# mLSTM attention with a mixture of experts: a unit's router logits move behind the scores of the iteration in which its rows are turned

## The chip, the cores and the metric

The kernel runs on one core of a Trainium2 chip. The metric is the device time of one execution in microseconds (us); runs of the same kernel differ by about two per cent, so medians are given with their spread.

## The reference

```python
for t in range(S):                       # B, H, S, D = 4, 8, 768, 40
    m_new = np.maximum(f[t] + m, i[t])
    f_stab, i_stab = np.exp(f[t] + m - m_new), np.exp(i[t] - m_new)
    C = f_stab * C + i_stab * outer(v[t], k[t]);  n = f_stab * n + i_stab * k[t];  m = m_new
    y[t] = sigmoid(o[t]) * (C @ q[t]) / max(abs(n @ q[t]), 1)
x = y as 3072 rows of 320 columns
noisy = x @ w_gate + log1p(exp(x @ w_noise)) * noise       # 8 experts
top2 = the two largest of each row; top2_w = softmax over the two
out[row] += top2_w * (relu(x[row] @ w1[e]) @ w2[e])        # for both experts e of a row
```

The recurrence is computed in chunks of 64 steps as scores, masked weights and a carried state.

## The kernel before, in words

**Attention.** The work is cut into NU = 24 units; a unit gives 128 rows of x. A loop runs over iterations i = 0 to 21, and the last two units are written out behind it. In iteration i, DVE makes `kd` (L340) and `p`, scores times weights (L346), of unit i+1; PE makes the state (`c_part`, L360), the output (`o_part`, L369) of unit i and the exponents of the weights of unit i+2 in two halves (`e_part`, L308), which ACT takes through exp (L311). `f_part` (L374 to L381) divides and gates unit i's output into `XR` on DVE and POOL. PE turns the rows of unit i-1 (`t_part`, L392, into the PSUM bank `xt`), ACT copies them to SBUF (`tc_part`, L396, tile `xts`), and PE makes the scores of unit i+2 (`s_part`, L329 and L332).

**Logits.** `l_part` (L412) multiplies a unit's turned rows with the router's weights, into columns of the same bank `xt`; `lc_part` (L461) copies the 16 logits of each row out of it on ACT.

**Routing.** Four units are a group; there are six. When a group's last logits are there, `route` starts `g_part`, a Python generator that emits the routing steps: noise and top two (L486 to L537), ranks inside an expert (`r_part` on PE, L421 to L423, copied by L464), places (L559 to L598), one-hot tiles `ob` (L604, eight for a group), and from them a burst of eight matmuls (`b_part`, L432) that adds the group's tokens to the token table (L439 or L442). `fill` decides how many steps of it go on DVE in each iteration; ranks and burst are due a fixed count of `unit` later (`lag`). Engines run their instructions in the order written. When three groups are in the table, `decode` (L448 to L452) makes the list of tokens for the first part of expert 0, and POOL gathers their rows (L743); after five groups that of the second part, after six that of the third and of expert 1.

**Experts.** Expert 0 is done in three parts as its tokens become known. `mm1` (L955) makes 128 hidden columns in a block, eight blocks for a part; ACT writes the relu (`hh`, L966), DVE the residue of its rounding (`hlo`, L967). `mm2` (L980 to L982) makes 128 rows of output from eight times three matmuls, one of the three with `hlo`. In the eight blocks of the first part ACT and POOL also split w2 (L756, L757), and the logits of the last units, their ranks and bursts are slipped in between (`advance`). `transpose_x` (L773 to L777) turns gathered rows. From expert 1 on, no routing is left.

## Time and profile before

| | us |
|---|---|
| median of three runs | 547.19 |
| lowest, highest | 539.72, 549.98 |
| the profiled execution, device time | 542.42 |
| its span, first to last instruction | 540.6 |
| PE busy, share of the span | 514.9, 95% |
| DVE busy, share of the span | 356.4, 66% |

The profiled execution lies between the lowest and the middle run. The page puts 71% of the chain that ended last on PE and 13% on DVE. PE's busy time is modelled for pipelined matmuls, so a high share does not say that PE is at its peak.

### The profile page before, as it was taken

To read this page: it belongs to the slowest core of one execution; us is meant where nothing else is said; L and a number is where in the kernel's file an instruction comes from. 1 tells how busy PE (TensorE), PEld (TensorE's weight loads), DVE (VectorE), ACT (ScalarE), POOL (GpSimd) and SP (SyncE) were. 2 spreads that over 40 slices of the span, in tenths; PEclk is the share of its full clock that TensorE was granted. 3 is DMA by queue.
4 is the path that set the end of the run, shared out by engine and by line. 5 is a ranking of instruction groups with operands and counts; after the bars stand their busy time and mean duration, and the time that the engine had idled before them with its cause. 6 is when DMAs were issued, how large, how long until landed. Compare 5 with 4: busy or idle time off the path is not lost.

```text
span 540.6 us, 13450 instructions
## 1 busy us (share of the span) xinstructions
PE 514.9 (95%) x5151; PEld 484.0 (90%) x5152; DVE 356.4 (66%) x956; ACT 248.7 (46%) x611; POOL 244.5 (45%) x329
## 2 busy tenths in 40 slices
PE   7999999999979899999999999999999999999992
PEld 3788888878978897899999999999999999999992
DVE  8898999998786368674675485467548537546310
ACT  7588878967532145451543254154326315515200
POOL 7446775644352854325705632570562345151042
PEclk9599999997989999999999999999999999999997
DMA  5889987788675455239417714941861583272032
GB/s 140 191 234 231 241 218 214 198 240 217 238 245 164 91 65 139 79 68 277 106 31 200 170 51 86 264 96 34 233 133 44 130 221 85 56 165 26 2 40 37
DMA packets 49990, 77.04 MB, mean 143 GB/s; under 512 B 10201, under 2 KB 39408, under 8 KB 49920
## 3 DMA queue, kind: packets, MB, share of 16 engines
q1 hardware_dynamic: 38848, 57.38, 37.6%
q0 software_dynamic: 11072, 18.74, 19.1%
q8 instruction: 42, 0.69, 0.5%
q14 instruction: 28, 0.23, 0.1%
HBM read 52.50 MB, written 17.48 MB: 129 GB/s over the span
## 4 chain that ended last, share of the span: by engine, by line
PE 71%; DVE 13%; DMA 5%; issue 3%; POOL 2%; ACT 2%; another core or an unknown queue 1%; SPq 1%; POOLq 0%; DVEq 0%
PE s L955 21%; PE e L955 11%; PE o L982 5%; PE o L980 5%; PE o L981 5%; PE st L980 4%; PE st L982 4%; PE st L981 4%; PE o L369 2%; DMA raw<-w_in 2%; DVE ob L604 2%; PE e L308 2%; DVE p L346 1%; PE s L332 1%
## 5 line engine op out<-in xcount | busy, mean ns | idle before, releaser
L1006 POOL DMA_INDIRECT y_out<-y,tok x54 | 88.7, 1643 | 191.7 <-DVE y L996 188.9
L966 ACT ACTIVATE hh<-s 128x384 fp32r<-128x384 f32 (+3 forms) x91 | 42.5, 469 | 84.7 <-PE s L955 75.8
L955 PE MATMUL s<-xh,w1h 128*128 128x384 f32 (+6 forms) x273 | 77.4, 338 | 0.1
L743 POOL DMA_INDIRECT xg<-rows,tok x54 | 60.9, 1127 | 26.0 <-issue 14.9
L967 DVE SCALAR_TENSOR_TENSOR hlo<-s,hh 128x384 fp32r<-128x384 f32 (+3 forms) x91 | 47.5, 522 | 28.5 <-ACT hh L966 25.1
L955 PE MATMUL s<-xh,w1l 128*128 128x384 f32 (+6 forms) x273 | 61.9, 335 | 0.0
L980 PE MATMUL o<-w2h,hh 128*128 128x320 f32 x192 | 59.5, 310 | 1.9 <-ACT hh L966 1.9
L982 PE MATMUL o<-w2h,hlo 128*128 128x320 f32 x192 | 59.2, 308 | 0.7 <-DVE hlo L967 0.7
L981 PE MATMUL o<-w2l,hh 128*128 128x320 f32 x192 | 58.7, 306 | 0.0
L980 PE MATMUL st<-w2h,hh 128*128 128x320 f32 x168 | 51.9, 309 | 0.0
L982 PE MATMUL st<-w2h,hlo 128*128 128x320 f32 x168 | 51.7, 307 | 0.0
L981 PE MATMUL st<-w2l,hh 128*128 128x320 f32 x168 | 51.4, 306 | 0.0
L955 PEld LDWEIGHTS s<-xh,w1h 128*128 128x128 f32 x273 | 49.2, 188 | 1.6 <-ACT xh L775 0.4
L955 PEld LDWEIGHTS s<-xh,w1l 128*128 128x128 f32 x273 | 47.8, 188 | 1.0
L955 PE MATMUL s<-xl,w1h 128*128 128x384 f32 (+6 forms) x182 | 46.3, 335 | 0.2 <-DVE xl L776 0.2
L996 DVE TENSOR_SCALAR y<-o,gw 128x320 f32<-128x320 f32 x24 | 13.2, 550 | 45.4 <-PE o L982 43.4
L966 ACT ACTIVATE hh<-e 128x384 fp32r<-128x384 f32 (+3 forms) x45 | 21.2, 472 | 40.6 <-PE e L955 40.1
L381 POOL TENSOR_TENSOR xr<-tm,vk 128x320 f32<-128x320 f32 x24 | 20.9, 872 | 40.0 <-PE e L308 8.4
L955 PE MATMUL e<-xh,w1h 128*128 128x384 f32 (+6 forms) x135 | 38.6, 340 | 0.3 <-DVE hlo L967 0.2
L996 DVE TENSOR_SCALAR y<-st,gw 128x320 f32<-128x320 f32 x21 | 11.6, 551 | 41.1 <-PE st L982 41.1
L980 PEld LDWEIGHTS o<-w2h,hh 128*128 128x128 f32 x192 | 36.0, 188 | 2.7 <-ACT hh L966 2.5
L982 PEld LDWEIGHTS o<-w2h,hlo 128*128 128x128 f32 x192 | 36.0, 188 | 1.1 <-DVE hlo L967 0.9
(233 smaller groups left out, 1323.0 us busy)
## 6 DMA issues: line engine op xcount, KB each, us to landing
vk<-vk_in SPq DMA_DIRECT2D x48, 242.0 KB
raw<-w_in SPq DMA_DIRECT2D x7, 1280.0 KB
qk<-qk_in SPq DMA_DIRECT2D x48, 160.0 KB
raw<-w_in SPq DMA_DIRECT2D x7, 1024.0 KB
y_out<-zrow SPq DMA_DIRECT2D x15, 320.0 KB
raw<-w_in SPq DMA_DIRECT2D x18, 256.0 KB
xt__2859<-xb SPq DMA_DIRECT2D x36, 72.0 KB
rows<-xr POOLq DMA_DIRECT2D x12, 160.0 KB
```

Source lines behind the costliest of these rows:

```text
L308: T.matmul(ps, LE[j][0:KE, c, 64 - 64 * p:192 - 64 * p], RE[j][0:KE, p, :, c * L:c * L + L], start=True, stop=True)
L369: T.matmul(OQ[u][half[p], h, :], PP[u][n, p, h, :], VK[u % 4][p][n, h * 41:h * 41 + 41], start=True, stop=True)
L381: P.tensor_mul(XR[u], tm.rearrange("p h d -> p (h d)"), SG[u % 4])
L743: P.indirect_dma_start(out=XG[0:rows_of(e, t), t], out_offset=None, in_=XD[0:n], in_offset=bass.IndirectOffsetOnAxis(ap=token(e, t), axis= ...
L955: T.matmul(ps[:, 0:n], l, r, start=i == 0, stop=i == len(ops) - 1)
L966: A.activation(hi, x, AF.Relu)
L967: V.scalar_tensor_tensor(lo, x, 0.0, hi.bitcast(F32), op0=OP.max, op1=OP.subtract)
L980: T.matmul(ps, HH[:, j, c], W2H[:, j], start=j == 0, stop=False)
L981: T.matmul(ps, HH[:, j, c], W2L[:, j], start=False, stop=False)
L982: T.matmul(ps, HLO[:, j, c], W2H[:, j], start=False, stop=j == 7)
L996: V.tensor_scalar(y[0:n], ps[0:n], GW[e][0:n, t:t + 1], None, op0=OP.mult)
L1006: st = P.indirect_dma_start(out=out, out_offset=bass.IndirectOffsetOnAxis(ap=token(e, t), axis=0), in_=y[0:n], in_offset=None, compute_op= ...
```

## The change: what it does

A unit's logits are made one iteration sooner. Before, iteration i made the logits of unit i-2, ahead of the turning of unit i-1; now it makes those of unit i-1, behind that turning, its copy and the scores of unit i+2. The ranks and bursts stay ahead of the turning. `route` starts a group one iteration sooner. Behind the loop, the logits of unit 21 stand where unit 22 is turned, those of unit 22 behind the first block of mm1 and those of unit 23 behind its fourth block instead of its third.

```diff
     def l_part(i):
-        t = XTB if i < NU else psum.tile([128, 512], F32, name="st")
-        u = i - 2
+        t = XTB if i < NU - 1 else psum.tile([128, 512], F32, name="st")
+        u = i - 1
...
     def lc_part(i, t, w):
-        u = i - 2
+        u = i - 1
...
     def route(i):
-        if 2 <= i <= NU + 1 and sum(GROUPS[GOF[i - 2]]) == i - 1:
-            routing.append(g_part(GOF[i - 2]))
+        if 1 <= i <= NU and sum(GROUPS[GOF[i - 1]]) == i:
+            routing.append(g_part(GOF[i - 1]))
...
         f_part(i, lambda: fill(0.15, False))
-        t = l_part(i)
-        w = r_part(t)
-        b = None if w else b_part(t)
+        w = r_part(XTB)
+        b = None if w else b_part(XTB)
+        lc_part(NU + 2, XTB, w)
+        bc_part(XTB, b)
         if i:
             t_part(i - 1)
             tc_part(i - 1)
-        lc_part(i, t, w)
-        bc_part(t, b)
         s_part(i + 2)
         act()
         sig_part(i + 1)
+        lc_part(i, l_part(i), None)
         e_part(i + LEAD, (1,))
         route(i)
...
-    t = l_part(u)
     t_part(u - 1)
     tc_part(u - 1)
-    lc_part(u, t, None)
     sig_part(u + 1)
     keep_rows(u)
     u = NU - 1
     o_room(u)
     o_part(u)
     f_part(u, lambda: None)
-    t = l_part(u)
+    lc_part(u - 1, l_part(u - 1), None)
     t_part(u - 1)
     tc_part(u - 1)
-    lc_part(u, t, None)
...
         if f == 0:
-            logits(NU)
+            logits(NU - 1)
         if f == 1:
             t_part(NU - 1)
             tc_part(NU - 1)
-        if f == 2:
-            logits(NU + 1)
+        if f == 3:
+            logits(NU)
```

**PE in one iteration of the loop.** Behind the first half of the exponents (L308) stands, before:

```order
L308 MATMUL e<-re_92,le_94 128x512
L412 MATMUL xt<-wgt,xts 128x16 x3
L392 MATMUL xt<-cs,xr 128x128 x3
L329 MATMUL s<-qk_100,cs 64x256 x2
L332 MATMUL s<-qk_100 64x64 x8
L329 MATMUL s<-qk_100,cs 64x256 x2
L332 MATMUL s<-qk_100 64x64 x8
L308 MATMUL e<-re_92,le_94 128x512
```

and now:

```order
L308 MATMUL e<-re_92,le_94 128x512
L392 MATMUL xt<-cs,xr 128x128 x3
L329 MATMUL s<-qk_100,cs 64x256 x2
L332 MATMUL s<-qk_100 64x64 x8
L329 MATMUL s<-qk_100,cs 64x256 x2
L332 MATMUL s<-qk_100 64x64 x8
L412 MATMUL xt<-wgt,xts 128x16 x3
L308 MATMUL e<-re_92,le_94 128x512
```

The logits (L412) have gone from ahead of the turning (L392) to behind the scores (L329, L332), and only the second half of the exponents still follows them.

**DVE from the `ob` tiles of the fifth group (units 16 to 19) to the token table (L439), in the first part of expert 0.** In the changed file L967 is L964. Before:

```order
L604 TENSOR_SCALAR ob<-cs,bi_3062 128x128 x6
L967 SCALAR_TENSOR_TENSOR hlo<-e,hh 128x384
L604 TENSOR_SCALAR ob<-cs,bi_3062 128x128 x2
L508 TENSOR_TENSOR nl_3103<-ln_2997,lg 128x32
L513 MAX mx_3105<-nl_3103 128x8 x4
L516 MAX_INDEX mi_3106<-mx_3105,nl_3103 128x8 x4
L523 TENSOR_TENSOR oh_3128<-cs,mi_3106 128x64
L529 TENSOR_TENSOR m_3134<-oh_3128 128x4x8
L534 COPY m_3134<-base_4_2987 128x8
L537 SCALAR_TENSOR_TENSOR base_4_3137<-anew_202,m_3134 128x40
L551 RECIPROCAL wts<-dd_3143 128x4
L439 TENSOR_TENSOR tbl<-tbl,o 128x56
```

and now:

```order
L604 TENSOR_SCALAR ob<-cs,bi_3017 128x128 x2
L486 SCALAR_TENSOR_TENSOR na_3059<-lg 128x32
L964 SCALAR_TENSOR_TENSOR hlo<-s_3067,hh 128x384
L495 SCALAR_TENSOR_TENSOR co_3082<-t_4_3062,ue_3061 128x32
L497 RECIPROCAL na_3059<-t_4_3062 128x32
L499 TENSOR_TENSOR co_3082<-co_3082,na_3059 128x32
L501 TENSOR_TENSOR ln_3063<-ln_3063,co_3082 128x32
L503 SCALAR_TENSOR_TENSOR ln_3063<-lg,ln_3063 128x32
L505 TENSOR_TENSOR ln_3063<-ln_3063,nzt 128x32
L508 TENSOR_TENSOR nl_3089<-ln_3063,lg 128x32
L964 SCALAR_TENSOR_TENSOR hlo<-e,hh 128x384
L439 TENSOR_TENSOR tbl<-tbl,o 128x56
```

The steps L513 to L551 of the sixth group, which stood ahead of the table, now stand behind it, behind the five steps of `decode` that follow L439; the sixth group's L486 to L508 stand ahead of it in both. In the new order the burst that the table waits for comes after the eighth block of mm1 and ahead of the first mm2, not inside that mm2.

**PE at the ranks of the sixth group (units 20 to 23), in the second mm2 of expert 0's first part.** In the changed file L980 to L982 are L977 to L979. Before:

```order
L982 MATMUL s_3183<-w2h,hlo 128x320
L980 MATMUL s_3183<-w2h,hh 128x320
L981 MATMUL s_3183<-w2l,hh 128x320
L982 MATMUL s_3183<-w2h,hlo 128x320
L421 LDWEIGHTS tri
L421 MATMUL o<-m_3134,tri 128x32
L422 LDWEIGHTS ones
L422 MATMUL o<-base_4_3137,ones 128x32
L423 LDWEIGHTS ones
L423 MATMUL o<-base_4_3137,ones 128x8
L980 MATMUL s_3183<-w2h,hh 128x320
L981 MATMUL s_3183<-w2l,hh 128x320
```

and now:

```order
L977 MATMUL s_3184<-w2h,hh 128x320
L978 MATMUL s_3184<-w2l,hh 128x320
L979 MATMUL s_3184<-w2h,hlo 128x320
L421 LDWEIGHTS tri
L421 MATMUL o<-m_3150,tri 128x32
L422 LDWEIGHTS ones
L422 MATMUL o<-base_4_3153,ones 128x32
L423 LDWEIGHTS ones
L423 MATMUL o<-base_4_3153,ones 128x8
L977 MATMUL s_3184<-w2h,hh 128x320
```

The ranks have moved from behind the third of this mm2's eight groups of three matmuls to behind its first.

## Rows read from the trace of the kernel before

**Rows 1.** The page, part 1: busy time, share of the span and instructions of each engine.

```profile
PE 514.9 (95%) x5151; PEld 484.0 (90%) x5152; DVE 356.4 (66%) x956; ACT 248.7 (46%) x611; POOL 244.5 (45%) x329
```

**Rows 2.** Busy time of each engine in five stretches (us from the start of the span; x counts instructions), with the granted clock and the DMA share: the loop, two stretches at a lower granted clock, the first expert block, and the experts later on.

```profile
86.00:112.00 26.00, 25.37 (x599) 22.18 (x594) 25.21 (x74) 20.52 (x55) 12.50 (x19) 1.00 0.74 200
...
121.20:128.00 6.80, 6.80 (x111) 5.75 (x108) 5.48 (x15) 4.38 (x12) 4.59 (x10) 0.57 1.04 253
...
137.50:158.70 21.20, 18.29 (x114) 16.90 (x112) 16.57 (x58) 9.01 (x30) 10.37 (x18) 0.98 0.73 248
158.70:165.60 6.90, 6.48 (x28) 6.16 (x29) 4.33 (x31) 0.94 (x3) 2.99 (x6) 0.57 0.98 271
...
400.00:500.00 100.00, 100.00 (x623) 99.88 (x622) 59.94 (x138) 41.22 (x97) 36.91 (x40) 1.00 0.46 104
```

**Rows 3.** Timeline of PE and ACT in one early iteration of the unit loop (start us, us, engine, line, operation, tiles, count, and idle time before with its releaser).

```profile
40.18 0.74 PE L412 MATMUL xt<-wgt,xts 128*128 128x16 f32 x6
40.38 0.60 ACT L311 ACTIVATE w<-e 128x512 f32<-128x512 f32 x1 [0.30 <-PE e L308]
...
40.77 0.52 PE L392 MATMUL xt<-cs,xr 128*128 128x128 f32 x3
...
41.33 0.49 ACT L396 ACTIVATE xts<-xt 128x384 f32<-128x384 f32 x1 [0.35 <-PE xt L392]
...
42.31 0.49 PE L308 MATMUL e<-re,le 98*128 98x512 f32 x1
```

**Rows 4.** Timeline of DVE: the product of scores and weights (L346) of two units that follow each other, later in the loop.

```profile
85.23 1.21 DVE L346 TENSOR_TENSOR p<-s,w 128x1024 f32<-128x1024 f32 x1
...
90.45 1.21 DVE L346 TENSOR_TENSOR p<-s,w 128x1024 f32<-128x1024 f32 x1
```

**Rows 5.** Timeline of all engines around the list of the first 12 units' tokens (L448 to L452), and the next two iterations.

```profile
115.04 1.32 POOL L148 TENSOR_TENSOR w1l<-raw,w1h 64x512 fp32r<-64x512 f32 x1 [1.08 <-issue]
...
115.12 1.27 DVE L450 TENSOR_SCALAR km<-tbl 128x3 f32<-128x3 f32 x1
...
116.38 0.16 DVE L452 TENSOR_SCALAR km<-tbl 128x3 f32<-128x3 f32 x1
...
119.59 1.75 PE L369 MATMUL o<-vk,p 104*64 104x41 f32 x32 [1.30 <-DVE mi L516]
...
121.75 1.22 DVE L346 TENSOR_TENSOR p<-s,w 128x1024 f32<-128x1024 f32 x1
...
128.01 1.22 DVE L346 TENSOR_TENSOR p<-s,w 128x1024 f32<-128x1024 f32 x1
```

**Rows 6.** Timeline of DVE in routing steps inside the loop: L495 to L499 of one group, and two L604 of a later one.

```profile
72.03 0.54 DVE L495 SCALAR_TENSOR_TENSOR co<-t,ue 128x32 f32<-128x32 f32 x1 [0.51 <-ACT t L673]
...
72.87 0.19 DVE L499 TENSOR_TENSOR co<-co,na 128x32 f32<-128x32 f32 x1
...
126.38 0.60 DVE L604 TENSOR_SCALAR ob<-cs,bi 128x128 fp32r<-128x128 f32 x2
```

**Rows 7.** Timeline of DVE and POOL in the first expert block, in the steps of the fourth group (L604) and the fifth (L486 to L499).

```profile
140.28 1.10 DVE L604 TENSOR_SCALAR ob<-cs,bi 128x128 fp32r<-128x128 f32 x2
...
141.30 0.18 DVE L486 SCALAR_TENSOR_TENSOR na<-lg 128x32 f32<-128x32 f32 x1
...
143.07 0.88 POOL L757 TENSOR_TENSOR w2l<-raw,w2h 128x320 fp32r<-128x320 f32 x1 [2.04 <-ACT w2h L756]
143.15 0.86 DVE L495 SCALAR_TENSOR_TENSOR co<-t,ue 128x32 f32<-128x32 f32 x1
...
144.19 0.88 POOL L757 TENSOR_TENSOR w2l<-raw,w2h 128x320 fp32r<-128x320 f32 x1 [0.24 <-ACT w2h L756]
144.30 0.81 DVE L499 TENSOR_TENSOR co<-co,na 128x32 f32<-128x32 f32 x1
```

**Rows 8.** Timeline of PE and DVE at the fifth group's burst (L432, eight matmuls), the first eight blocks' last residue (L967), the sixth group's steps (L513 to L537), the token table (L439) and the gather of the second part's rows (POOL L743).

```profile
157.02 0.46 PE L432 MATMUL o<-oa,ob 128*128 128x56 f32 x2 [1.31 <-DVE ob L604]
...
158.00 0.41 PE L432 MATMUL o<-oa,ob 128*128 128x56 f32 x1 [0.52 <-DVE ob L604]
...
158.82 0.93 PE L432 MATMUL o<-oa,ob 128*128 128x56 f32 x3 [0.41 <-DVE ob L604]
159.20 0.55 DVE L967 SCALAR_TENSOR_TENSOR hlo<-e,hh 128x384 fp32r<-128x384 f32 x1
...
160.05 0.67 PE L432 MATMUL o<-oa,ob 128*128 128x56 f32 x2 [0.31 <-DVE ob L604]
...
160.38 0.37 DVE L513 MAX8 mx<-nl 128x8 f32<-128x8 f32 x4
...
162.22 0.18 DVE L439 TENSOR_TENSOR tbl<-tbl,o 128x56 f32<-128x56 f32 x1
...
163.20 1.09 POOL L743 DMA_INDIRECT xg<-rows,tok  x1 [0.60 <-DMA raw<-w_in]
```

**Rows 9.** Timeline of PE from the sixth group's ranks (L421) over the transposes of the gathered rows (L773) to the first mm1 of the second part (L955) and a burst whose operands lay ready.

```profile
164.69 0.20 PE L421 MATMUL o<-m,tri 128*128 128x32 bf16 x1
...
169.88 0.55 PE L773 MATMUL s<-cs,xg 128*128 128x128 f32 x3 [0.45 <-DMA xg<-rows,tok]
...
172.22 0.51 PE L955 MATMUL s<-xh,w1h 128*128 128x256 f32 x2
...
173.87 0.97 PE L432 MATMUL o<-oa,ob 128*128 128x56 f32 x8
```

## The prediction

> **What bounds the kernel now.** I read the page's busy times first [rows 1]: PE is busy for 95% of the span, so a change that leaves the work as it is can only win where PE waits or runs at a lower clock. The busy times by stretch [rows 2] say where that is. From 400 to 500 us PE is busy for all of the 100 us: whatever is won or lost ahead of expert 1 comes out at the end unchanged. In the loop, from 86 to 112 us, DVE is busy for 25.21 of 26 us, and one unit takes 5.22 us [rows 4]: the loop is DVE's once routing steps are in it. In the first expert block, 137.5 to 158.7 us, PE is idle for 2.9 of 21.2 us, and behind it, from 158.7 to 165.6 us, the granted clock is 0.57. The timeline there [rows 8] shows why: the fifth group's burst waits four times for DVE's one-hot tiles, 1.31, 0.52, 0.41 and 0.31 us, then the table (L439) comes at 162.22, the gather at 163.20, and its rows are turned at 169.88 after another wait of 0.45 [rows 9]. In this stretch the routing on DVE decides, not PE's work.
>
> **Logits behind the scores.** The same three matmuls and the same copy are issued; only their place changes. PE's logits take 0.59 us, from 40.18 to the turning at 40.77 [rows 3]; that moves from ahead of the turning to behind the scores, and the second half of the exponents, which PE reaches at 42.31, keeps its time if no wait is added. There is a new one: the logits need ACT's copy of rows turned in the same iteration. Queued behind them on PE are these exponents and then the next unit's state and output; DVE's next product waits for the exponents through ACT. On ACT the logits' copy now stands between the gate's three steps and the exponents' exp, and waits for PE. From the rows: turning and scores start 0.59 earlier, the turning ends at 40.70; ACT is in its exp until 40.98 and copies until 41.47; the scores end at 42.31 - 0.59 = 41.72. The copy is hidden with 0.25 us to spare: I cost the wait at nothing. If the cover is gone, each of 21 iterations pays the excess.
>
> **Routing one iteration sooner, in the loop.** The loop now also does the fourth group's last two L604 and the fifth's L486 to L499. At the loop's own prices these are 0.60, 0.18 (this one from [rows 7]) and, from 72.03 to 73.06, 1.03 us [rows 6], so 1.8; at the prices in the first expert block they are 1.10 + 0.18 + (145.11 - 143.15 = 1.96) = 3.2 [rows 7]. DVE bounds the loop, so this is on the path. The list of the first tokens comes at the start of iteration 18 rather than 19. Before, its L450 took 1.27 us against 0.16 for L452 of the same size, and ended with POOL's split of w1 [rows 5]; this split is issued at the end of even iterations, so an odd iteration's end has none: 1.1 us less. The loop's sum is 1.8 - 1.1 = +0.7. Two ends: +3.2 if the dearer prices hold and another step meets POOL instead; and 0.7 - 1.0 = -0.3 if PE's wait of 1.30 us at 119.59, after which the granted clock fell to 0.57 [rows 2, 5], goes with it, since the unit behind it took 128.01 - 121.75 = 6.26 us, 1.0 over the ordinary 5.22. I take +0.7, the clock left as it was.
>
> **The first expert block.** Ahead of the table on DVE go: the 3.2 us of moved steps [rows 7], the fourth group's L439 at 0.2 (the price of the one in [rows 8]), and the sixth group's L513 to L551, which now come behind the table, 162.22 - 160.38 = 1.8 [rows 8]. That is 5.3 us (3.24 + 0.18 + 1.84): the table at 156.9 instead of 162.22. Does PE follow? The last residue, 0.55 us [rows 8], now ends just ahead of it, at 156.9 too, and the first mm2's last matmuls need it, so PE is at its second mm2 at about 157.3. One group of three matmuls costs 0.47 (from 164.69 to 169.88 less the wait of 0.45, ten of them [rows 9]), so it could make the ranks at 157.8. But the sixth group's L537 is not there: 156.9, 1.0 for the list (162.22 to 163.20), 1.8 for the steps, gives 159.7. PE waits 1.9 us, with the rest of this mm2 queued behind. The ranks come at 159.7 instead of 164.69, 5.0 sooner. From ranks to the first mm1 of the second part it was 172.22 - 164.69 = 7.53, of it 0.45 wait; now two more groups of three stand there (0.9) and no wait, 8.0, and the sixth burst stands ahead of this mm1 instead of behind its first block, 0.97 either way [rows 9]. The gather, 5.3 us sooner on POOL, lands at 169.88 - 5.3 = 164.6, and is wanted at 159.7 + 12 x 0.47 = 165.3, so it is hidden. The burst stands 8 us behind the ranks; eight L604 at 0.55 (half of 1.10, [rows 7]) and some 2 us of steps before them fit. So the second part starts at 159.7 + 8.0 + 1.0 = 168.7 instead of 172.22 + 0.97 = 173.2: **4.5 us sooner**. Ends: 6.4 if the 1.9 us wait is not there either; 1.5 if PE, after this wait, runs all 6.9 us at 0.57 once more without any of it falling on time in which it waits for DVE anyway (6.9 x 0.43 = 3.0 [rows 2]). The middle is nearest the rows, since its waits, some 2 us, are about those that there were.
>
> The sixth group's logits, a block later, cost nothing: its steps end behind the fifth's on DVE in both orders, and what waits for them is the ranks in the sum above.
>
> The Trainium skill, page "SBUF — State Buffer", section "Who interferes with whom", says that a DVE step with two SBUF inputs contends with a GpSimd step that reads SBUF, and that the one issued second is blocked whole. The trace agrees in two places [rows 7]: L495 ends at 144.01 with POOL's split at 143.95, and L499 at 145.11 with the next at 145.07, 0.81 long against 0.19 in [rows 6]. The rule speaks against counting the full 3.2 us; the second rival below goes by it.
>
> **The sum.** +0.7 - 4.5 = -3.8 us on the profiled execution of 542.42: 538.6. The median of before is 547.19, 4.8 above that execution, and I carry the difference over: **543.4**. The ends are 542.42 - 0.3 - 6.4 = 535.7 (540.5 in terms of the median) and 542.42 + 3.2 - 1.5 = 544.1 (548.9).
>
> **Rivals.** *Scores too short (slower).* ACT comes to the copy later than in [rows 3], for instance behind the copies of ranks and bursts, which keep their place ahead of it, and PE stands at the logits. The spare is 0.25 us. At 0.5 us lost in each of 21 iterations the loop pays 10.5: -3.8 + 10.5 = +6.7, 553.9. From a loss of 0.18 on the change is slower. Against it: ACT was idle for 0.35 us ahead of the copy [rows 3], and later the loop waits for DVE, which hides PE's waits. *POOL takes the time from other steps.* The eight splits of w2 stay in the first expert block, and the steps that stand beside them now are blocked like L495 and L499: of the 3.2 us only the 1.8 are won, the tail gives 3.1 and the whole 2.4: 544.8. For it: both blocked steps end with POOL [rows 7]; against: L604 lost time there as well and has other neighbours now. *Nothing is left.* The loop pays 3.2 and the clock takes 3.0: 548.9 as above; the waits in the block, not their length, would decide that. *DVE is caught up (more).* The granted clock stays up in the loop and in the block and PE waits for nothing there: 540.5 or a little less. That the change does not do what it says can be left out: the order shows it on each engine.
>
> **How the numbers follow.** Chances: the forecast 0.42, POOL's splits 0.22, nothing left 0.15, caught up 0.13, slower by the scores 0.08. The likeliest is 543.4. The cases reach from 540 to 549; the three runs of before, 539.72 to 549.98, spread as wide, and a median of three can lie some 5 us off on its own, so I give 534 to 550, wider below because the profiled execution lies low already. Two per cent, 11 us, is about what a measurement of this kernel can tell from no change. Faster by more needs the last-but-one case and a lucky spread: 0.07; slower by more only the first rival at its full price: 0.05; within it 0.88.
>
> **What would show it.** In the changed profile: the gather of the second part's rows some 5 us sooner against the end of attention, with no wait of PE for it; PE's four waits at the burst gone or short, and a wait of about 2 us at the ranks in the second mm2; the first mm1 of the second part 4 to 5 us sooner; one unit in the loop still about 5.2 us, PE with no waits for ACT's copy at the logits, and attention's end within 1 us of before; L450 at about 0.2 us. The prediction is wrong if the logits show waits for the copy in most iterations, if attention ends 2 us or more later, or if low granted clock covers a longer time than the two stretches of before.

## The result and the profile after

The changed kernel is **slower**: 551.29 us (median of 20 runs, 545.84 to 563.81) against 544.82 (20 runs, 539.72 to 550.62) of the kernel before beside it. The ratio is 1.0115, 95% interval 1.0086 to 1.0145: less than the two per cent by which single runs differ, but clear of the noise of 20. The forecast was 543.4, 0.7% below the 547.19 then known, with a range of 534 to 550. Every ratio and mean from here on leaves out the runs over 1.5% above the fastest of the same kernel, while the expectations from e10 on speak of means over all runs, with more time lost to the clock. The profiled execution has a span of 547.6 us, 7.0 more than before.

The page, part 1, of the kernel after, against [rows 1]: the work is the same, PE is busy for 2.6 us more.

```profile
PE 517.5 (94%) x5151; PEld 486.5 (89%) x5152; DVE 355.4 (65%) x955; ACT 250.8 (46%) x612; POOL 244.1 (45%) x330
```

Where the 7 us come from is seen by stretches. First the first product of expert 0 on PE, before and after:

```profile
137.50 0.59 PE L955 MATMUL s<-xh,w1h 128*128 128x384 f32 x2
```

```profile
145.42 0.60 PE L952 MATMUL s<-xh,w1h 128*128 128x384 f32 x2
```

Then the loop, from 30 us to the first product of expert 0, of the kernel before; then the same of the kernel after, and a part of it (columns as in [rows 2]).

```profile
30.00:137.50 107.50, 104.05 (x2383) 90.74 (x2379) 99.83 (x283) 85.54 (x219) 61.72 (x109) 0.97 0.83 219
```

```profile
30.00:145.40 115.40, 107.58 (x2355) 93.11 (x2354) 101.52 (x286) 87.52 (x221) 61.50 (x109) 0.94 0.75 204
...
88.70:102.80 14.10, 14.10 (x210) 12.30 (x201) 9.62 (x35) 8.13 (x21) 3.89 (x7) 0.52 0.66 183
```

The loop is 7.9 us longer. On PE that is idle time, which went from 3.45 us (107.50 - 104.05) to 7.82, and busy time, which grew by 3.53 although the work is the same, since the granted clock is at its half level for 14 us from 88.7 on. Before, the one such stretch in the loop was 6.8 us long [rows 2]. DVE's work in the loop has grown by 1.69 us (101.52 less 99.83), where the forecast's two terms add up to 0.7.

The waits of PE in the loop, of the kernel after (engine, tile and line waited at, releaser: us in total, times, longest):

```profile
PE xt L392 <- ACT rk L464: 3.5, 4, 1.0
...
PE xt L392 <- ACT share L441: 1.6, 4, 0.4
PE o L369 <- DVE tm L380: 0.7, 1, 0.7
PE xt L432 <- DVE ob L604: 0.6, 1, 0.6
PE xt L392 <- ACT lg L461: 0.4, 1, 0.4
```

and all of the kernel before:

```profile
PE o L369 <- DVE mi L516: 1.3, 1, 1.3
PE e L308 <- ACT w L311: 0.7, 1, 0.7
PE s L332 <- issue: 0.6, 1, 0.6
PE o L369 <- DVE tm L380: 0.6, 2, 0.4
PE st L360 <- issue: 0.2, 1, 0.2
```

The first two lines of the kernel after, eight waits and 5.1 us, have no counterpart before. L392 is the turning of the rows; L464 and L441 are ACT's copies of the ranks and of the bursts. The timeline of PE and ACT shows one of them, and then the place ahead of the low clock:

```profile
54.01 0.17 PE L423 MATMUL xt<-base,ones 128*128 128x8 bf16 x1
55.17 0.52 PE L392 MATMUL xt<-cs,xr 128*128 128x128 f32 x3 [0.98 <-ACT rk L464]
...
86.37 0.84 PE L432 MATMUL xt<-oa,ob 128*128 128x56 f32 x3 [0.64 <-DVE ob L604]
87.61 0.52 PE L392 MATMUL xt<-cs,xr 128*128 128x128 f32 x3 [0.40 <-ACT share L441]
```

```profile
53.57 0.89 ACT L363 ACTIVATE vk<-st 40x328 f32<-40x328 f32 x2
54.36 0.58 ACT L311 ACTIVATE w<-e 128x512 f32<-128x512 f32 x1
54.83 0.19 ACT L464 ACTIVATE rk<-xt 128x40 f32<-128x40 f32 x1
```

PE has the ranks at 54.2 and turns at 55.17, when ACT's copy ends (54.83 + 0.19), which stands behind the state's copies and an exp. In the change's code `lc_part(NU + 2, XTB, w)` and `bc_part(XTB, b)` stand ahead of `t_part`; before, they stood behind it. The turning writes the PSUM tile that they read, so it must let them read first. The program orders the two by the whole tile, although their columns are others.

The Trainium skill, page "PSUM — Partial Sum Buffer", section "PSUM bank collisions raise a hardware error", says why nothing else would do: two engines must not touch the same bank and quadrant at once, whichever columns, so accesses are to be guarded by bank and not by address. The trace shows what this order costs, here a wait of 0.98 us between other columns of one bank; no run here let the two overlap.

The rest of the program, of the kernel after, answers to [rows 3, 5, 8, 9] (PE, DVE and POOL; first the logits in an early iteration and ACT's copy for them, then the token list, then the first expert block):

```profile
39.76 0.48 ACT L396 ACTIVATE xts<-xt 128x384 f32<-128x384 f32 x1
...
40.58 0.84 PE L412 MATMUL xt<-wgt,xts 128*128 128x16 f32 x6
```

```profile
118.11 0.16 DVE L450 TENSOR_SCALAR km<-tbl 128x3 f32<-128x3 f32 x1
```

```profile
158.36 1.17 PE L432 MATMUL o<-oa,ob 128*128 128x56 f32 x6
159.96 0.55 PE L432 MATMUL o<-oa,ob 128*128 128x56 f32 x2 [0.43 <-DVE ob L604]
...
164.94 0.20 DVE L439 TENSOR_TENSOR tbl<-tbl,o 128x56 f32<-128x56 f32 x1
165.89 1.09 POOL L743 DMA_INDIRECT xg<-rows,tok  x1 [2.29 <-DVE mx L513]
...
165.08 0.41 PE L979 MATMUL s<-w2h,hlo 128*128 128x320 f32 x1 [1.01 <-DVE hlo L964]
...
167.10 0.18 PE L421 MATMUL o<-m,tri 128*128 128x32 bf16 x1 [1.17 <-DVE m L534]
...
174.28 0.49 PE L773 MATMUL s<-cs,xg 128*128 128x128 f32 x3
...
177.06 0.48 PE L952 MATMUL s<-xh,w1h 128*128 128x256 f32 x2
```

The first product of expert 0 starts at 145.42 (before: 137.50), that of its second part at 177.06 (172.22). The block between them is 31.6 us instead of 34.7. So 7.9 us are lost in the loop and 3.1 won back. A further 2.2 are lost behind it, where the clock stood low once more for 6.8 us from 191.8 on, with 0.54 granted.

### The profile page after: what moved, and what is told of

It is laid out like the page before. It is cut to its first block, busy times and chain, and to the rows that moved or that the text cites. A ratio compares the mean times of both kernels' runs of the same rounds, so it can differ in the third digit from the quotient of the medians.

```text
span 547.6 us, 13461 instructions
## 1 busy us (share of the span) xinstructions
PE 517.5 (94%) x5151; PEld 486.5 (89%) x5152; DVE 355.4 (65%) x955; ACT 250.8 (46%) x612; POOL 244.1 (45%) x330
## 3 DMA queue, kind: packets, MB, share of 16 engines
q0 software_dynamic: 11072, 18.74, 18.2%
## 4 chain that ended last, share of the span: by engine, by line
PE 71%; DVE 16%; DMA 4%; issue 3%; POOL 2%; ACT 2%; SPq 0%; another core or an unknown queue 0%; POOLq 0%; DVEq 0%
PE s L952 21%; PE e L952 10%; PE o L977 5%; PE o L979 5%; PE o L978 5%; PE st L977 5%; PE st L979 5%; PE st L978 5%; DVE p L346 3%; DVE ob L604 2%; DVE kd L340 2%; PE o L369 1%; DVE tm L380 1%; PE xt L412 1%; PE st L360 1%
## 5 line engine op out<-in xcount | busy, mean ns | idle before, releaser
L743 POOL DMA_INDIRECT xg<-rows,tok x54 | 60.1, 1113 | 27.5 <-issue 14.9
L964 DVE SCALAR_TENSOR_TENSOR hlo<-s,hh 128x384 fp32r<-128x384 f32 (+3 forms) x91 | 47.5, 522 | 29.7 <-ACT hh L963 23.2
L977 PE MATMUL o<-w2h,hh 128*128 128x320 f32 x192 | 59.8, 312 | 3.5 <-issue 2.0
L979 PE MATMUL o<-w2h,hlo 128*128 128x320 f32 x192 | 59.5, 310 | 0.7 <-DVE hlo L964 0.7
L977 PE MATMUL st<-w2h,hh 128*128 128x320 f32 x168 | 52.8, 314 | 0.0
L979 PE MATMUL st<-w2h,hlo 128*128 128x320 f32 x168 | 52.4, 312 | 0.0
L381 POOL TENSOR_TENSOR xr<-tm,vk 128x320 f32<-128x320 f32 x24 | 21.1, 879 | 43.2 <-DVE tm L380 13.7
L977 PEld LDWEIGHTS o<-w2h,hh 128*128 128x128 f32 x192 | 36.1, 188 | 4.5 <-issue 2.2
L979 PEld LDWEIGHTS o<-w2h,hlo 128*128 128x128 f32 x192 | 36.1, 188 | 1.1 <-DVE hlo L964 0.9
```

The lines of the kernel that those rows point to most:

```text
L381: P.tensor_mul(XR[u], tm.rearrange("p h d -> p (h d)"), SG[u % 4])
L743: P.indirect_dma_start(out=XG[0:rows_of(e, t), t], out_offset=None, in_=XD[0:n], in_offset=bass.IndirectOffsetOnAxis(ap=token(e, t), axis= ...
L964: V.scalar_tensor_tensor(lo, x, 0.0, hi.bitcast(F32), op0=OP.max, op1=OP.subtract)
L977: T.matmul(ps, HH[:, j, c], W2H[:, j], start=j == 0, stop=False)
L979: T.matmul(ps, HLO[:, j, c], W2H[:, j], start=False, stop=j == 7)
```

## The experiments

Each ratio is to the kernel before on the same chip. Two numbers beside it split the time, worked out for each run from its span S and the mean clock g that the run was granted: S times g, what the program would take at full clock if all of it went with the clock, and S times (1 - g), the time lost to the clock. They are means, and a microsecond or two uncertain; the ratios on record are not quotients of these means and differ from them by up to 0.25%. The changed kernel has 531.8 and 16.3; of the kernel before beside it only the profiled execution's clock is on record.

The split counts low clock wherever it stands, ahead of the loop too, where it cost little. The two profiled executions show it: 523.3 and 17.3 before (540.6 us at 0.968), 531.7 and 15.9 after (547.6 at 0.971). By the split alone the clock would have no part in their 7 us. But the kernel before had 13.6 us of its low clock from 14.5 us on, the kernel after 3.4 from 20.5 on, and the same unit's product (L346) starts at 30.92 and at 30.57 us, almost alike. In the loop it is the kernel after whose clock is lower, 0.94 against 0.97.

| run | ratio [95%] | S g, this / before | S (1-g), this / before |
|---|---|---|---|
| e1 | 1.0052 [1.0010, 1.0093] | 524.5 / 525.3 | 16.4 / 13.1 |
| e2 | 1.0073 [1.0039, 1.0106] | 524.3 / 525.3 | 17.4 / 13.1 |
| e4 | 1.0150 [1.0092, 1.0208] | 527.8 / 525.3 | 18.2 / 13.1 |
| e5 | 1.0027 [0.9985, 1.0069] | 526.4 / 525.3 | 12.8 / 13.1 |
| e6 | 1.0049 [0.9997, 1.0102] | 528.4 / 528.3 | 16.4 / 13.6 |
| e7 | 1.0067 [1.0016, 1.0118] | 528.8 / 528.3 | 17.4 / 13.6 |
| e8 | 1.0081 [1.0035, 1.0128] | 528.5 / 528.3 | 18.4 / 13.6 |
| e9 | 1.0029 [0.9997, 1.0060] | 528.7 / 528.3 | 15.1 / 13.6 |
| e10 | 1.0141 [1.0084, 1.0199] | 525.0 / 525.6 | 20.2 / 12.5 |
| e11 | 1.0038 [1.0003, 1.0073] | 526.5 / 525.6 | 13.4 / 12.5 |
| e12 | 1.0201 [1.0146, 1.0256] | 527.8 / 525.6 | 20.0 / 12.5 |
| e13 | 1.0128 [1.0090, 1.0166] | 528.8 / 525.0 | 14.7 / 12.2 |
| e14 | 1.0207 [1.0154, 1.0260] | 524.0 / 525.0 | 24.6 / 12.2 |
| e15 | 1.0164 [1.0110, 1.0219] | 526.7 / 525.0 | 19.5 / 12.2 |
| e16 | 1.0107 [1.0055, 1.0159] | 528.0 / 525.0 | 16.2 / 12.2 |
| e17 | 1.0102 [1.0059, 1.0145] | 525.9 / 527.8 | 21.5 / 14.1 |
| e18 | 1.0012 [0.9970, 1.0054] | 528.4 / 527.8 | 14.0 / 14.1 |

The letters of the theories hold within a group of runs. The waits named below are of PE in the loop.

**The change in parts.** e1 is the changed kernel with the copies back behind the turning; e2 is the kernel before with the copies alone put ahead; e4 is the changed kernel with the routing started as late as before in the loop; e5 is e1 with that edit too, so that only the logits have moved.

```diff
 e1, against the changed kernel
-        lc_part(NU + 2, XTB, w)
-        bc_part(XTB, b)
         if i:
             t_part(i - 1)
             tc_part(i - 1)
+        lc_part(NU + 2, XTB, w)
+        bc_part(XTB, b)
 e2, against the kernel before
+        lc_part(NU + 2, t, w)
+        bc_part(t, b)
         if i:
             t_part(i - 1)
             tc_part(i - 1)
-        lc_part(i, t, w)
-        bc_part(t, b)
+        lc_part(i, t, None)
 e4 against the changed kernel, e5 against e1: in route(i)
-        if 1 <= i <= NU and sum(GROUPS[GOF[i - 1]]) == i:
-            routing.append(g_part(GOF[i - 1]))
+        late = 1 if i < NU else 0
+        u = i - 1 - late
+        if 0 <= u < NU and sum(GROUPS[GOF[u]]) == u + 1:
+            routing.append(g_part(GOF[u]))
```

e1: 

> The changed kernel, with one thing put back: ACT's copies of ranks and bursts (L464, L441) are written behind the turning and its copy again, as before the change; logits stay behind the scores and routing stays one iteration sooner. Theory A (the turning, L392, waits for these copies, since they read the same PSUM tile and now stand ahead of it; 5.1 us in eight waits in the changed trace, and PE's clock falls behind them): no waits of L392 for L464 or L441, the first mm1 of expert 0 at 137 to 140 us instead of 145.4, and the 4.5 us gained in the first expert block are left: ratio to before 0.990 to 0.996. Theory B (the routing moved into the loop makes DVE the bound there and costs the loss): the first mm1 stays at 144 to 146, ratio 1.008 to 1.015. Theory C (the logits wait for the copy of the turned rows): as B, with waits at L412.

e2: 

> The kernel before, with only this: ACT's copies of ranks and bursts are written ahead of the turning. Nothing else moves: logits ahead of the turning, routing as late as before. Theory A: seven turnings in the loop wait for the copies, 4 to 5 us in all, and the clock may fall behind some of them: ratio 1.006 to 1.015. Theories B and C: no logits behind scores and no routing moved, so 0.998 to 1.002.

e4: 

> The changed kernel, with a group's routing started one iteration later in the loop, as before the change; the logits stay behind the scores and the copies ahead of the turning. Theory A: the waits of L392 stay and the gain in the first expert block goes: ratio 1.010 to 1.020, the worst of these runs. Theory B: the loop is as before: 0.998 to 1.002. Theory C: 1.008 to 1.015.

e5: 

> Only the logits are moved behind the scores: copies of ranks and bursts behind the turning as before, and routing started as late as before. What the move of the logits costs by itself. Theory A and B: 0.998 to 1.002. Theory C: 1.008 to 1.015, with waits at L412.

Measured: 1.0052, 1.0073, 1.0150, 1.0027. e2 and e4 lie in theory A's ranges and e5 just above its 1.002; e1, for which it had 0.990 to 0.996, does not fit it. The copies ahead of the turning cost 0.7% in the kernel before (e2, where seven turnings wait for them, 4.5 us in all) and 1.2% between e5 and e4. The place of the logits alone costs nothing that can be measured (e5). The cause at the turning is plain in PE's timeline, first of the kernel before, then of e2, where the same two instructions follow each other:

```profile
59.13 0.17 PE L423 MATMUL xt<-base,ones 128*128 128x8 bf16 x1
59.15 0.52 PE L392 MATMUL xt<-cs,xr 128*128 128x128 f32 x3
```

```profile
59.14 0.17 PE L423 MATMUL xt<-base,ones 128*128 128x8 bf16 x1
59.98 0.52 PE L392 MATMUL xt<-cs,xr 128*128 128x128 f32 x3 [0.67 <-ACT rk L464]
```

But e1, without these waits and with the routing sooner, did not win what the first expert block gives: its block is 31.7 us long, as after, and yet its first product of expert 0 comes at 146.1 us, not at 137 to 140, and it lies 0.5% above before. Its timeline shows a wait of another kind, in the fourth group's iteration (POOL, DVE, PE):

```profile
124.45 1.26 POOL L148 TENSOR_TENSOR w1l<-raw,w1h 64x512 fp32r<-64x512 f32 x1 [4.31 <-DMA vk<-vk_in]
...
127.10 0.23 POOL L546 TENSOR_SCALAR dd<-d 128x4 f32<-128x4 f32 x1
```

```profile
127.37 0.18 DVE L551 RECIPROCAL wts<-dd 128x4 f32<-128x4 f32 x1 [5.31 <-POOL dd L546]
```

```profile
128.28 1.93 PE L369 MATMUL o<-vk,p 104*64 104x41 f32 x32 [4.08 <-DVE rk L559]
```

A routing step of DVE reads a sum that POOL makes; POOL stood at its split of w1 until a transfer landed; PE stood 4.08 us behind DVE.

**Is it this one wait?** e6 puts the fourth group's routing alone back; e7 (e1), e8 (the changed kernel) and e9 (the kernel before) make the sum of L546 on DVE.

```diff
 e6, against e1
-        if 1 <= i <= NU and sum(GROUPS[GOF[i - 1]]) == i:
-            routing.append(g_part(GOF[i - 1]))
+        late = 1 if 16 <= i <= 17 else 0
+        u = i - 1 - late
+        if 0 <= u < NU and sum(GROUPS[GOF[u]]) == u + 1 and (i != 16):
+            routing.append(g_part(GOF[u]))
 e7, e8, e9: in g_part
-        P.tensor_scalar(dd, d, 1.0, 1e-9, op0=OP.add, op1=OP.add)
+        V.tensor_scalar(dd, d, 1.0, 1e-9, op0=OP.add, op1=OP.add)
```

e6: 

> The kernel with the copies of ranks and bursts back behind the turning, and the routing sooner for five of the six groups; only the fourth group (units 12 to 15) starts its routing as late as in the kernel before. In the run with all six sooner (542.95, ratio 1.0052), the DVE stood 5.31 us ahead of the reciprocal of L551 of that group, because the sum of L546 on POOL that it reads stood behind the split of L148, which waited 4.31 us for the weights' transfer; PE waited 4.08 us for the DVE there, and the clock was low afterwards. Theory B (this one wait eats what the first expert block gains): wait and low clock are gone, ratio 0.988 to 0.997, that is 534 to 539 us; the transposes at L773 start by 138. Theory C (the DVE is full in the loop, so what is moved into it comes out at its end, wherever it stands): 1.000 to 1.008, 540.5 to 545 us.

e7: 

> The copies of ranks and bursts back behind the turning, routing sooner for all groups, and the sum of L546 written on the DVE instead of POOL, so that the reciprocal of L551 behind it waits for nothing of POOL's. Theory B (the wait of L551 for POOL's queue eats the gain): no idle time of the DVE at L551, 0.2 us more DVE work in each group, ratio 0.988 to 0.997 (534 to 539 us), about as with the fourth group alone put back. Theory C (the DVE is full): 1.000 to 1.010 (540.5 to 546 us), a little slower for the six added operations.

e8: 

> The changed kernel with one edit, the sum of L546 on the DVE. The changed kernel waits there 5.4 us in all on the DVE, 2.9 at most in one wait inside the loop. Theory A (the copies ahead of the turning make the loss; the waits of L392 for them stay): 1.006 to 1.012, 543.5 to 547 us, nearly as slow as the changed kernel (1.0115). Theory B (the wait for POOL's sum makes the larger part): 0.992 to 1.003, 536 to 542 us.

e9: 

> The kernel before with the sum of L546 on the DVE and nothing else: a control for the two runs with that edit. Its trace has no wait of L551 for L546 in the loop, so every theory gives 0.997 to 1.003 (539 to 542.5 us); if it is as fast as the run with the sooner routing and this edit, the gain there is not the routing's.

Measured: 1.0049, 1.0067, 1.0081, 1.0029. Theory B fell: no trace of e6 to e8 has a wait of PE like that of 4.08, and the lost time stays. The ratios of e6 and e7 lie in theory C's ranges, that of e8 in theory A's. But e7 and e8 differ in the copies alone, and their ratios by 0.14%, far inside the intervals: with the routing sooner on this chip, the price of the copies is not seen. In e6 another wait does its work (PE's timeline, then two stretches):

```profile
65.89 0.87 PE L432 MATMUL xt<-oa,ob 128*128 128x56 f32 x4 [1.18 <-DVE ob L604]
```

```profile
60.00:67.70 7.70, 6.52 (x137) 5.62 (x137) 7.63 (x14) 5.08 (x13) 6.20 (x11) 0.95 0.91 235
67.70:77.90 10.20, 10.20 (x149) 8.99 (x143) 7.49 (x31) 6.12 (x17) 4.53 (x9) 0.54 0.72 193
```

A burst is asked of PE one iteration after it is announced, and with the routing sooner DVE had not written `ob` by then. PE waited 1.18 us, and the clock stood at half for the next 10.2 us, some 5 us of PE's work. The table says the same of all three: S g as before, 2.8 to 4.8 us more lost to the clock. So the next question was the clock.

**The price of a wait, and orders without waits.** e12 is the kernel before with DVE's product repeated in three iterations. e10 and e11 move the bursts' products, or these and the ranks', behind the scores. e13 and e14 move them behind the logits; e15 is e13 with the routing late. All but e12 have the sum on DVE, and the copies behind the turning.

```diff
 e12, against the kernel before
         p_part(i + 1)
+        if i in (8, 13, 18):
+            for _ in range(2):
+                V.tensor_mul(PP[i + 1], SQ[i + 1], W[i + 1])
 e10, against e7 (e11: w = r_part and lc_part(NU + 2, ...) move too)
         w = r_part(XTB)
-        b = None if w else b_part(XTB)
...
         lc_part(NU + 2, XTB, w)
-        bc_part(XTB, b)
         s_part(i + 2)
+        b = None if w else b_part(XTB)
         act()
         sig_part(i + 1)
+        bc_part(XTB, b)
         lc_part(i, l_part(i), None)
 e13, against e7 (e14: the lines of w stay; e15: also route(i) as in e4)
-        w = r_part(XTB)
-        b = None if w else b_part(XTB)
...
-        lc_part(NU + 2, XTB, w)
-        bc_part(XTB, b)
         s_part(i + 2)
         act()
         sig_part(i + 1)
         lc_part(i, l_part(i), None)
+        w = r_part(XTB)
+        b = None if w else b_part(XTB)
+        lc_part(NU + 2, XTB, w)
+        bc_part(XTB, b)
```

e10: 

> The kernel of the run with the sum on the DVE (copies behind the turning, routing sooner, L546 on the DVE), and the bursts' products (L432) behind the scores, so that the DVE has some 1.8 us more to write ob before PE asks for it. In that run PE waited 1.39 us at 65.2 for ob and the granted clock stood at half from 66.9 for 44.4 us; span times one minus the mean granted clock, the time lost to the clock, was 26.2 us in the mean of its 14 runs, against 14.3 in 35 of the kernel before. Theory D (what the sooner routing costs is the clock that falls behind a wait of PE of half to one and a half microseconds, not the waits themselves): no wait at L432 in the loop, time lost to the clock 13 to 18 us in the mean, ratio 0.990 to 1.000 (538 to 544 us where the kernel before takes 544). Theory C (the DVE is full, and the work comes out at the loop's end; the clock is chance): lost time as before the edit, 20 to 27, ratio 1.002 to 1.012.

e11: 

> As the run with the bursts behind the scores, and the products of the ranks (L421 to L423) behind the scores too. This takes away the wait of PE for base at L422 (1.11 us at 75.9 in the run with only the copies put back), but the ranks reach the DVE some 1.8 us later, and the DVE, which is the engine that the loop's units share last, may stand at L559 for them. Theory D: time lost to the clock 13 to 18 us; by the DVE's wait at L559 (up to 2 us in each of five groups) the work, span times clock, is 0 to 4 us over the run before it; ratio 0.990 to 1.005. Theory C: 1.002 to 1.012.

e12: 

> The price of a wait by itself. The kernel before, and in three iterations (8, 13 and 18) the multiplication of L346 written twice more with the same operands and result: 1.22 us each, 2.4 us of the DVE in each of the three, 7.3 us in all. The DVE is busy 19 of 20 us in the loop, so PE will wait for it some 1 to 2.4 us in each of these places. Theory D (the granted clock falls behind such waits): time lost to the clock grows by 3 to 12 us over the 14 of the kernel before, the ratio is 1.010 to 1.035, and the clock's falls begin within 3 us of the waits. Theory C (the clock is chance and knows nothing of the waits): lost time 12 to 16 us as before, all of the difference in span times clock, 3 to 7 us; ratio 1.005 to 1.013.

e13: 

> Routing sooner, L546 on the DVE, and in each iteration on PE: turning, scores, logits, and only then the products of ranks or bursts (L421 to L423, L432), their copies on ACT last. No matmul of the same iteration follows on the tile that these copies read, and the DVE has some 2.5 us more before PE asks. Theory D (the clock falls behind PE's waits): no wait of PE for base, ob, rk or share in the loop; time lost to the clock 11 to 16 us in the mean of the runs, where the kernel before loses 13 to 14 and the variants with sooner routing lost 17 to 26; the first expert block keeps its 3 us; ratio 0.988 to 0.999. Theory C (no room on the DVE): 1.002 to 1.010, the waits of PE at L369 for the DVE, longer, in place of those taken away.

e14: 

> As the run before it, but the ranks' products stay ahead of the turning, with their copy behind the turning's, so that the ranks come to the DVE as soon as in the kernel before; only the bursts stand behind the logits. Theory D: PE waits up to 1.1 us at L422 for base in some groups and 0.5 at L412 for the ranks' copy, so the lost time is 13 to 18 us; ratio 0.990 to 1.003. Theory C: 1.002 to 1.010.

e15: 

> The order of the run with everything asked behind the logits, but the routing starts as late as in the kernel before while the loop runs: the control that tells what the order alone is worth. Both theories: the first expert block is as long as before (34.7 to 35.2 us from its first product to the first of the second part), ratio 0.995 to 1.004. If it is as fast as the run with the sooner routing, the sooner routing is worth nothing even without waits.

Measured for e12: 1.0201; the means differ by 9.7 us. Of the 7.3 us of added DVE work S g shows 2.2; the time lost to the clock grew by 7.5, as theory D had it (3 to 12). Its timeline and stretches:

```profile
92.33 1.13 PE L369 MATMUL o<-vk,p 104*64 104x41 f32 x32 [2.54 <-DVE tm L380]
```

```profile
88.00:94.30 6.30, 3.76 (x97) 3.22 (x89) 6.16 (x13) 2.94 (x9) 2.65 (x4) 0.94 0.52 148
94.30:101.10 6.80, 6.80 (x97) 5.92 (x96) 4.57 (x17) 3.73 (x12) 1.17 (x2) 0.56 0.65 184
```

The orders e10 to e15 did not do what I expected of them: 1.0141, 1.0038, 1.0128, 1.0207, 1.0164; all but e11 lie above the ranges of both theories. Each put a new wait on the same tile. In e10 and e11 the logits wait for the burst's copy (0.31 to 1.90 us at L412), in e11 for the ranks' too (0.93 to 1.23); in e13 to e15 the burst waits for the logits' copy, as here in e13 (PE, ACT, stretches):

```profile
89.42 0.84 PE L412 MATMUL xt<-wgt,xts 128*128 128x16 f32 x6
92.30 1.05 PE L432 MATMUL xt<-oa,ob 128*128 128x56 f32 x4 [2.04 <-ACT lg L461]
```

```profile
92.08 0.17 ACT L461 ACTIVATE lg<-xt 128x16 f32<-128x16 f32 x1
```

```profile
92.20:99.00 6.80, 6.70 (x87) 5.83 (x91) 5.98 (x26) 2.22 (x6) 1.18 (x3) 0.55 0.62 176
```

e15, with the routing late and such a wait of 0.95 us at each of three bursts, loses as much (1.0164): what costs the time in these orders does not need the sooner routing. e11's 1.0038 fits either theory.

**Last runs.** e16 keeps the changed kernel's copies ahead of the turning and gives PE half of the scores to do meanwhile. e17 puts ranks and bursts on the PSUM tile of the carried state; e18 is e17 with the routing late.

```diff
 e16, against the changed kernel (s_part takes a range of heads)
+        n = 4 if w or b else 0
+        s_part(i + 2, range(n))
         if i:
             t_part(i - 1)
             tc_part(i - 1)
-        s_part(i + 2)
+        s_part(i + 2, range(n, 8))
 e17, against e7 (e18: also route(i) as in e4)
+        asks = [a for a in (want[0:1] and want[0][5], bursts[0:1] and bursts[0][2]) if a and a <= unit[0]]
+        rb = psum.tile([128, 512], F32, name="st") if asks else None
-        w = r_part(XTB)
-        b = None if w else b_part(XTB)
         if i:
             t_part(i - 1)
             tc_part(i - 1)
-        lc_part(NU + 2, XTB, w)
-        bc_part(XTB, b)
+        w = r_part(rb)
+        lc_part(NU + 2, rb, w)
         s_part(i + 2)
+        b = None if w else b_part(rb)
         act()
         sig_part(i + 1)
+        bc_part(rb, b)
```

e16: 

> The changed kernel with one edit: in an iteration with ranks or a burst, the first half of the scores (four of eight heads, some 0.7 us of PE) stands between their products and the turning, so that PE has work while ACT copies them; the copies stay ahead of the turning. Theory A with D (the waits of L392 for these copies and the clock behind them make the change's loss): the eight waits of 0.4 to 1.0 us at L392 fall to 0 to 0.4, the time lost to the clock from 19.1 to 14 to 17 us, ratio 0.998 to 1.006. If the loss is in the sooner routing and not in these waits: 1.008 to 1.014, as the changed kernel.

e17: 

> Routing sooner, L546 on the DVE, and the products of ranks and bursts on the PSUM tile of the carried state (st, which is free after the copies of L363) in place of the turning's (xt): ranks behind the turning, bursts behind the scores. No matmul on the turning's tile waits for a copy of theirs any more, and the DVE has 0.5 us more before the ranks and 1.8 before the bursts are asked for. Theory D: PE's waits in the loop at L392, L412, L421, L422 and L432 are all under 0.6 us, the time lost to the clock is 11 to 16 us (13 to 14 in the kernel before), the first expert block keeps its 3 us, ratio 0.988 to 0.999. Theory C: the waits come at L369 for the DVE instead, ratio 1.002 to 1.010.

e18: 

> The same with the routing started as late as in the kernel before while the loop runs: the control. Both theories: first expert block 34.7 to 35.2 us, time lost to the clock 12 to 15 us, ratio 0.996 to 1.004; the sooner routing is worth what lies between this run and the one before it (theory D: -0.5 to -0.9%, theory C: 0 to +0.6%).

Measured: 1.0107, 1.0102, 1.0012. e16's ratio is the one that its expectation gave to a loss in the sooner routing and not in the copies. PE's waits at L392 for the copies fell from 5.1 to 1.2 us, but in its trace DVE stands 4.87 us at L551 for POOL's sum, as in e1, PE behind DVE, and the clock falls behind that (PE, then two stretches):

```profile
128.12 1.10 PE L369 MATMUL o<-vk,p 104*64 104x41 f32 x31 [2.82 <-DVE rk L559]
```

```profile
122.00:130.60 8.60, 5.50 (x109) 4.49 (x112) 3.56 (x13) 4.24 (x12) 5.07 (x10) 0.95 0.74 176
130.60:151.10 20.50, 20.50 (x277) 18.25 (x269) 12.65 (x31) 10.36 (x27) 3.81 (x6) 0.52 0.39 110
```

e17 kept two waits of nearly 1 us, one for DVE (L369, 0.95, from theory C's list) and one for the burst's copy (L360, 0.92), and its ratio is about C's (up to 1.010). The waits that theory D named for it (L392, L412, L421, L422, L432) are under 0.6 us, as it asked, and yet the lost time is 21.5, not 11 to 16: to take away the waits at one tile was not enough. In S g it lies 2.5 us below e18, about what the first expert block gives; in the time lost to the clock 7.5 above. e1 against e5, one chip as well, says 1.9 below and 3.6 above. e13 against e15 does not fit (2.1 above in S g), so this split is not settled.

## Why the prediction was wrong

- **The step that failed** is the first: "the same three matmuls and the same copy are issued; only their place changes". The copies of ranks and bursts change their place too. The prediction saw them ("the copies of ranks and bursts, which keep their place ahead of it") and meant their place ahead of the logits' copy on ACT; it missed that they now stood ahead of the turning, and that PE's turning waits for them on the shared tile. Eight waits, 5.1 us, in the profile; e2 and e4 against e5 show their price, 0.7 and 1.2%. They are not the whole: without them the sooner routing still lies 0.5% above before (e1) and not 0.7% below, and e7 against e8 shows no price for them. The rest is the loop's term below.
- **The logits behind the scores** cost nothing that e5 can measure, as forecast: the copy ends 0.34 us ahead of them in the early iteration shown, no wait of 0.25 us or more stands at L412 in the loop (one turning behind it waits 0.36 us for their copy, L461), and e5 measures 1.0027 with an interval that holds 1. The rival of the scores too short did not happen, though the sum it gave, 553.9, is nearer to the result.
- **The loop's term** was +0.7, with ends -0.3 and +3.2. L450 took 0.16 us, as forecast. But DVE's work grew by 1.7 us with that saving of 1.1 in it, so its other steps grew by 2.8, not 1.8, nearer to the dear end: L561, for one, took 0.95 us in two groups where 0.27 stood before. That is 1 us more than the term had; the loop was 7.9 us longer. "The clock left as it was" failed (13.7 us at half in the loop, 6.8 before), and the term had no place for a wait of PE for DVE or POOL that the shifted steps bring (1.18 at L432 in e6, 4.08 at L369 in e1).
- **The first expert block** held: 3.1 us shorter, with a burst of about 1 us ahead of the second part that stood behind before, so about 4 like for like, against 4.5. The wait at the ranks was 1.17 us (and one of 1.0 at the last residue ahead of it) where 1.9 was forecast, the gather was hidden, and of the four waits at the burst one of 0.43 was left.
- **The sum** was made of a block's gain, which is real, and of a loop costed at its work. That the loop's price lies in waits, and in the clock behind them, was in the data: before, the one wait of 1.30 us at 119.59 stood ahead of 6.8 us at 0.57 [rows 2, 5]. The prediction used that only as an end on the good side. Some 2.4 us of its distance are the base: the median of three runs that it started from, 547.19, lay that far above the median of 20.

What stays open: which wait is followed by a low clock. No run isolated the sooner routing without waits of PE, so what it would be worth then is not measured. None of the seventeen beat the kernel before. An estimate can be had from single executions, the traces of all kernels but e7, e11, e14 and e15. In the eight with the routing sooner (e6 for five groups of six) the first product of expert 0 comes at 147.1 us in the mean, in the seven with it late at 139.8. Less half of the time at the half level since 30 us, which is the most that the low clock can have cost, these are 137.7 and 136.9. The first expert block takes 30.0 to 32.7 us in the eight and 34.7 to 35.2 in the seven. By this estimate the loop's loss is nearly all clock, and the sooner routing would be worth some 2 to 4 us if the clock stayed up; no run shows that.

## What to carry to other kernels

When a block is moved in the code, list every read and write of the tiles that it shares, and ask which other engine's read now stands ahead of a write of the engine that sets the time: a copy moved by three lines cost 0.7% by itself here (e2), and the logits that the change was about nothing that could be measured (e5). In a loop where PE is nearly always busy, price a new wait of PE at what the clock did behind the waits that the trace already has, and not at its own length. A gain read in one block is not a gain until the queue that pays for it has been followed wait by wait.

## What the runs showed of the hardware

The granted clock fell behind waits of PE. In the fifteen traces other than those of e7, e11, e14 and e15 (before and after counted in) there are 23 falls to the half level (1.2 GHz) between 42 and 152 us; in the 2.5 us ahead of 22 of them, or at their start, PE had stood idle for 0.4 us or more, most often at one wait (two of the 22 rest on idle times without a releaser in the trace, where records can be missing). That is not chance: only 20% of the time at full clock lies so close behind such an idle time. In the other four traces it is 10 of 11 falls. The low stretches lasted 3.4 to 23.9 us in the fifteen, up to 44.4 in the four. It is not a rule for each wait: such a stretch began in or behind seven of the eight waits of more than 1.6 us with a releaser in the trace, and behind fifteen of the 98 shorter ones (down to 0.25); the kernel e18 waited 1.04 and 1.77 us for a transfer and kept its clock. e12 is the one run that added only work of DVE, and it lost more to the clock than to the work; that the waits cause the falls rests on it and on the order in time, and is not shown beyond that. Where a stretch followed, PE lost up to half of it, 1.7 to 12 us, on top of a wait of 0.4 to 4.1 us.

The Trainium skill, page "TensorE: Matmul & The Clock Gate", section "A second HAM failure mode: psum-queue depth-cycling", tells of a kernel whose TensorE idles briefly between groups of matmuls so often that its clock swings between the two levels. The traces agree in kind: ahead of e6's fall PE stood still once, for 1.18 us, and then had the half level for 10.2.
